# Two chained MLPs behind a small convolution: the two VectorE passes of a step put together, side work spread wider, six blocks in front

## The chip, the cores and the metric

One core of a Trainium2 chip runs the whole program. The metric is the device time of one execution in microseconds (us); smaller is better. Of the kernel before, three runs are shown (1156.45 to 1156.87 us) beside one profiled execution.

## The reference

`x` is 2 x 4096 x 192, `weight_gen` 2 x 4096 x 8 x 7, both float32. Each of the 8192 tokens gets a softmax over 7 taps in 8 heads, and a causal sum of the last 7 tokens with these taps. Two MLPs follow, each 192 to 2048 to 192 wide:

```python
w = np.exp(weight_gen - weight_gen.max(-1, keepdims=True)); w /= w.sum(-1, keepdims=True) + 1e-9
x = np.einsum('bshk,bskhg->bshg', w, x_unf).reshape(8192, 192)
h = np.maximum(x @ w_in, 0);  x = (h * h) @ w_out
h = x @ w2_in;  out = (h * np.clip(h + 3, 0, 6) / 6) @ w2_out
```

## The kernel before, in words

Every float32 operand of a matmul is split in a high part, which TensorE takes exactly, and a low part, and three products (high x high, high x low, low x high) make one result. Tokens go in 16 blocks of 512, the 2048 hidden columns in 16 tiles of 128. A *unit* is one block, one MLP and one hidden tile; two units make a *step* (`FG = 2`), eight steps one MLP of one block. `units` is the order: first `LEAD` blocks of the first MLP, then by turns one block of the second MLP and one of the first, at the end the `LEAD` blocks of the second MLP that are left. That is 32 stretches of eight steps, 256 steps.

In a step TensorE (`emit_pair`, all matmuls at L335) multiplies into `h` of the new unit pair, 9 pairs of matmuls that run side by side on the halves of the array, and mixes in the 10 pairs with which the pair of three steps earlier (`LAG = 6` units) goes through the second matrix into `accN` and `accR`. Behind it, per pair of units:

- `emit_E1` on ScalarE reads `h`: the first MLP's relu (L419) and square (L420), the second MLP's relu of h + 3 (L422). It writes `g`.
- `emit_V1` on VectorE, second MLP alone: g = min(g, 6) * h (L428).
- `emit_E2` on ScalarE: the high part `gh` of `g` (L433).
- `emit_V2` on VectorE: the low part `gl` = g - gh (L439). `g`, `gh`, `gl` and the PSUM tile `h` have two buffers each.

E1 and V1 of a pair are issued one step behind its matmuls, E2 and V2 two steps behind, and TensorE takes `gh` and `gl` in the step after that.

Besides, VectorE and ScalarE do side work. A *conversion* of a weight group (256 hidden columns, eight groups per MLP) splits the raw weights: `weight_head` (VectorE L119, then ScalarE L123, L124) and the four operations o2 to o5 of `weight_ops` (VectorE L137, L142, L149, L154; behind L142 the ScalarE casts L145, L146). A *convolution* of a block is a softmax for every second block (L204 to L220, with an exp on ScalarE, L208), thirteen products and sums (L235, L248), and a transpose (L314) whose result goes through DRAM: SyncE stores it (L318), and `from_dram` loads it as `x` (L306). Then `split_1` (ScalarE, L268) and `split_2` (VectorE, L273) make the halves `sh` and `sl`, at fixed places: six and four units ahead of the block's start. `finish` (L447) empties the accumulators. Conversions and convolutions are lists of jobs with due times. `run_jobs` hands out the next operations by estimated costs, `UNIT` per step less what is fixed; when a job is due it is issued whatever it costs. ScalarE operations that follow from a job are put off with `later` to the end of the step (`flush`).

The order within a step stands in the loop at L685 to L703:

```python
emit_E1(*units[i - FG])
emit_E2(*units[i - 2 * FG])
emit_V1(*units[i - FG])
...   # operations at fixed places, run_jobs(i)
emit_V2(*units[i - 2 * FG])
```

SyncE issues nearly all DMAs in one queue in program order; a DMA whose data is not ready keeps those behind it waiting.

Of the kernel before, what the change touches and what calls it, by code (L numbers as in the profile page):

```python
# [18 lines left out]
def conv_moe_moe2_kernel(  # L19
# [26 lines left out]
    NK = D // HP  # L46
    DR = D - P
    LAG = 6
    LEAD = 4

    xf = x.rearrange("b s d -> (b s) d")
    wf = wgen.rearrange("b s h k -> (b s) (h k)")
# [20 lines left out]
    FG = 2  # L73
# [120 lines left out]
    def load_rest():  # L194
        nc.sync.dma_start(out=wc[0][:, TB:, :], in_=w_v[:, TB:CT, :])
        nc.sync.dma_start(out=xc[0][:, PAD + TB:, :], in_=x_v[:, TB:CT, :])

    def softmax_ops(c, t0=0, t1=CT):
        e = wc[c][:, t0:t1, :].rearrange("p t (h k) -> p (t h) k", k=K)
        n = (t1 - t0) * H  # L200
        st = att.tile([P, CT * H, 2], F32, tag="pr", name="st", bufs=2)[:, 0:n, :]

        def o1():
            nc.vector.tensor_reduce(out=st[:, :, 0:1], in_=e, axis=AX.X, op=ALU.max)  # L204

        def o2():
            nc.vector.tensor_tensor(out=e, in0=e, in1=st[:, :, 0:1].to_broadcast([P, n, K]), op=ALU.subtract)
            later(lambda: nc.scalar.activation(e, e, AF.Exp))  # L208

        def o3():  # L210
            nc.vector.tensor_reduce(out=st[:, :, 1:2], in_=e, axis=AX.X, op=ALU.add)

        def o4():
            nc.vector.tensor_scalar_add(st[:, :, 1:2], st[:, :, 1:2], 1e-9)

        def o5():
            nc.vector.reciprocal(out=st[:, :, 0:1], in_=st[:, :, 1:2])

        def o6():
            nc.vector.tensor_tensor(out=e, in0=e, in1=st[:, :, 0:1].to_broadcast([P, n, K]), op=ALU.mult)  # L220

        return [(o, .45) for o in (o1, o2, o3, o4, o5, o6)]
# [44 lines left out]
    def split_1(m, b):  # L267
        nc.scalar.copy(halves(m, b)[0], xraw[m, b][:, 0:NK])  # L268

    def split_2(m, b):  # L270
        src = xraw.pop((m, b))[:, 0:NK]
        hi, lo = xs_in[m, b]
        nc.vector.tensor_tensor(out=lo, in0=src, in1=hi.bitcast(F32), op=ALU.subtract)  # L273

    def x_tile():
        return act.tile([P, NK + 1, N], F32, tag="x", name="x")
# [24 lines left out]
    def from_dram(m, b):  # L301
        Sf = xdram.pop((m, b))
        x = xraw[m, b] = x_tile()
        n = NK + m
        for h in range(2):
            nc.sync.dma_start(  # L306
                out=x[h * HP:(h + 1) * HP, 0:n], in_=Sf[0:n * HP].rearrange("(j p) n -> p j n", p=HP)
            )

    def transpose_dma(b):  # L310
        a = attn.pop(b)
        S = scr.tile([D, Q, P], F32, tag="xs", name="xs")
        aT = att.tile([P, J, TB, 32], F32, tag="pr", name="aT", bufs=2)
        nc.vector.transpose(  # L314
            out=aT.rearrange("p j t c -> p t j c"), in_=a.rearrange("p t (j c) -> p t j c", j=J)
        )
        for q in range(Q):
            nc.sync.dma_start(  # L318
                out=S[:, q, :].rearrange("(j c) n -> c j n", c=32),
                in_=aT[q * 32:(q + 1) * 32].rearrange("p j t c -> p j (t c)"),  # L320
            )
        xdram[0, b] = S.rearrange("d q n -> d (q n)")
        at.setdefault(max(unit_now[0] + 2, start_of[0, b] - 12), []).insert(0, lambda: from_dram(0, b))

    freed = []

# [88 lines left out]
    def emit_E1(m, b, f):  # L415
        ps = h_ps[m, b, f]
        g = g_sb[m, b, f] = gp.tile([P, FG, N], F32, tag="g", name="g")
        if m == 0:
            nc.scalar.activation(g, ps, AF.Relu)  # L419
            nc.scalar.activation(g, g, AF.Square)  # L420
        else:
            nc.scalar.activation(g, ps, AF.Relu, bias=3.0)  # L422

    def emit_V1(m, b, f):
        ps = h_ps.pop((m, b, f))
        if m == 1:
            g = g_sb[m, b, f]
            nc.vector.scalar_tensor_tensor(out=g, in0=g, scalar=6.0, in1=ps, op0=ALU.min, op1=ALU.mult)  # L428

    def emit_E2(m, b, f):  # L430
        g = g_sb[m, b, f]
        gh = gp.tile([P, FG, N], F32R, tag="gh", name="gh")
        nc.scalar.copy(gh, g)  # L433
        g_sb[m, b, f] = gh, g

    def emit_V2(m, b, f):
        gh, g = g_sb[m, b, f]
        gl = gp.tile([P, FG, N], F32R, tag="gl", name="gl")
        nc.vector.tensor_tensor(out=gl, in0=g, in1=gh.bitcast(F32), op=ALU.subtract)  # L439
        g_sb[m, b, f] = gh, gl  # L440
# [13 lines left out]
    def finish_1(b):  # L454
        z = zsum.pop((0, b))
        S = scr.tile([2 * P, N], F32, tag="ys", name="ys", bufs=LEAD + 1)
        for o in (1, 0):
# [73 lines left out]

    stages = [(0, b) for b in range(LEAD)]
    for b in range(LEAD, NB):
        stages += [(1, b - LEAD), (0, b)]
    stages += [(1, b) for b in range(NB - LEAD, NB)]
    units = [(m, b, f) for m, b in stages for f in range(NF)]
    NU = len(units)
    unit_of = {u: i for i, u in enumerate(units)}
    start_of = {(m, b): unit_of[m, b, 0] for m in range(2) for b in range(NB)}
# [13 lines left out]
    for u, (m, b, f) in enumerate(units):  # L553
        need.setdefault((m, f // FG), u)

    UNIT, UNIT2, AHEAD, DEBT = 4.45, 3.8, 8, 1
    COST = {0: 1.25, 1: 2.45}
    at, load = {}, {}

    def put(u, op, cost=0):  # L560
        at.setdefault(u, []).append(op)
        load[u] = load.get(u, 0) + cost
# [3 lines left out]
    def job(kind, make, due, release=0):  # L566
        jobs[kind].append([due, release, make, None, False])
# [3 lines left out]
    def weight_job(i):  # L571
        ops = weight_ops(*groups[i])
        if i + 2 < len(groups):
            ops.insert(2, (lambda: load_weights(*groups[i + 2]), 0))
        if i + 1 < len(groups):
            ops.insert(-1, (lambda: weight_head(*groups[i + 1]), .6))
        if i + 1 == len(groups):
            ops.append((lambda: freed.append(True), 0))
        return ops

    def conv_job(b):
        c, t0 = divmod(b * TB, CT)
        ops = []
        if b == 1:
            ops += softmax_ops(0, TB, CT)
        elif t0 == 0:
            ops += softmax_ops(c)
        ops += conv_ops(b)
        if t0 and b + 1 < NB:
            ops.append((lambda: load_chunk(c + 1), 0))  # L590
        ops.append((lambda: transpose_dma(b), 1))
        ops.append((lambda: ended_at.append(unit_now[0]), 0))
        return ops
# [11 lines left out]
    unit_now = [0]  # L605
# [32 lines left out]

    for i in range(1, len(groups)):
        job("w", lambda i=i: weight_job(i), need[groups[i]] - FG)  # L640
    job("a", lambda: conv_job(1), start_of[0, 1] - 10)
    for b in range(1, NB):

        if b > 1:
            rel = max(start_of[0, b - 1] + 2, end_of[0, b - 2] - 6)
            due = start_of[0, b] - (12 if b <= LEAD else 10)
            job("a", lambda b=b: conv_job(b), due, (rel, b, start_of[0, b - 1] - 8))
        put(start_of[0, b] - 6, lambda b=b: split_1(0, b))
        put(start_of[0, b] - 4, lambda b=b: split_2(0, b), 1.75)
# [14 lines left out]
    with tc.manual_schedule():  # L664
        load_chunk(0)
        load_weights(0, 0)
        load_rest()
        nc.gpsimd.memset(tiny, 0.0)
        nc.scalar.activation(tiny, tiny, AF.Exp)
        load_weights(0, 1)  # L670
        make_identity(nc, ident)
        c0 = conv_ops(0)
        steps = softmax_ops(0, 0, TB) + c0[:-2] + [(lambda: weight_head(0, 0), 0)] + c0[-2:]
        for op, _ in steps:
            op()
            flush()
        w0 = weight_job(0)

        steps = [(lambda: transpose_pe(0), 0)] + w0[1:4] + w0[:1]
        steps += [(lambda: split_pe(0), 0)] + w0[5:] + w0[4:5]  # L680
        for op, _ in steps:
            op()
            flush()

        for i in range(0, NU + LAG, FG):  # L685
            if i < NU or i in second:
                emit_pair(units[i] if i < NU else None, second.get(i))
            if 0 <= i - FG < NU:
                emit_E1(*units[i - FG])
            if 0 <= i - 2 * FG < NU:  # L690
                emit_E2(*units[i - 2 * FG])
            if 0 <= i - FG < NU:
                emit_V1(*units[i - FG])
            for u in range(i, i + FG):
                for op in at.get(u, []):
                    op()
            run_jobs(i)
            if 0 <= i - 2 * FG < NU:
                emit_V2(*units[i - 2 * FG])
            m, b, f = second.get(i - FG, (0, 0, 0))  # L700
            if f + FG == NF and (m, b) != units[-1][:2]:
                finish(m, b)
            flush()  # L703
        finish_last(NB - 1)
# [30 lines left out]
```

## Time and profile before

| | |
|---|---|
| three runs | 1156.45, 1156.47 (median), 1156.87 us |
| profiled execution | 1157.02 us, span 1155.2 us, mean granted TensorE clock 0.984 |
| TensorE busy | 1097.3 us, 95% |
| VectorE busy | 825.8 us, 71% |
| ScalarE busy | 769.9 us, 67% |
| DMA | 87.90 MB, mean 76 GB/s |

The span runs from the first to the last instruction; the profiled execution's own time lies 1.8 us above it. Busy shares are means over stages that differ: a start without matmuls, a front in which weights are converted, a long middle, and an end.

### The profile page before, as it was taken

The numbers are of one execution on the slowest core, as the hardware profiler recorded it, in microseconds if no ns is written. First come the engines' busy times: TensorE is split into PE (matmuls) and PEld (weight loads), VectorE is DVE, ScalarE is ACT, GpSimd is POOL, SyncE is SP. The second block draws the span as 40 slices with busy tenths as digits, with TensorE's granted clock in tenths as the row PEclk, the third lists the DMA queues.
The fourth block names the chain that finished last, engine by engine and source line by source line (L and its number), as shares of the span: only waits on it lengthen the run. The fifth ranks groups of instructions, "written<-read, shape, count | busy, mean of one in ns | idle before, by whom it ended". The sixth has DMA issues, their size and how long they took to land.

```text
span 1155.2 us, 23575 instructions
## 1 busy us (share of the span) xinstructions
PE 1097.3 (95%) x9722; PEld 922.9 (80%) x9722; DVE 825.8 (71%) x839; ACT 769.9 (67%) x829; POOL 3.3 (0%) x11
## 2 busy tenths in 40 slices
PE   2679999999999999999999999999999999999998
PEld 1457777788878888888888888888888888888886
DVE  8969897785777767776686857767677766366665
ACT  3677889576676757667575765757567575756553
POOL 0000000000000000000000000000000000000000
PEclk9679999999999999999999999999999999999999
DMA  5552534024113322314202241143223132022211
GB/s 137 162 127 60 168 95 114 20 65 130 37 47 93 98 60 51 87 39 139 56 28 74 53 142 37 42 96 98 60 49 90 38 84 56 28 69 51 74 42 47
DMA packets 68755, 87.90 MB, mean 76 GB/s; under 512 B 5612, under 2 KB 44396, under 8 KB 67752
## 3 DMA queue, kind: packets, MB, share of 16 engines
q1 hardware_dynamic: 68504, 86.19, 28.0%
q8 instruction: 77, 1.26, 0.5%
q14 instruction: 30, 0.25, 0.1%
q10 hardware_dynamic: 144, 0.20, 0.0%
HBM read 59.89 MB, written 26.48 MB: 75 GB/s over the span
## 4 chain that ended last, share of the span: by engine, by line
PE 76%; DVE 10%; ACT 7%; issue 3%; DMA 2%; SPq 1%; DVEq 0%; ACTq 0%
PE h L335 35%; PE accN L335 24%; PE accR L335 17%; DVE gl L439 3%; DVE pr L235 2%; ACT g L419 2%; ACT gh L433 2%; DVE a L248 2%; ACT g L420 1%; DMA st<-in_moe_w_out_dram 1%; DVE w L154 1%; DMA xs<-aT 0%; DVE hb L142 0%; ACT q L123 0%; ACT t L124 0%
## 5 line engine op out<-in xcount | busy, mean ns | idle before, releaser
L335 PE MATMUL h<-sh,w 64*128 64x512 f32 x3072 | 615.9, 381 | 19.1 <-DVE w L154 8.8
L335 PE MATMUL accN<-gh,w 64*128 64x512 f32 x2024 | 522.3, 378 | 0.3 <-ACT gh L433 0.3
L335 PE MATMUL h<-sl,w 64*128 64x512 f32 x1536 | 443.1, 380 | 0.0
L335 PEld LDWEIGHTS h<-sh,w 64*128 64x128 f32 x3072 | 386.1, 188 | 68.9 <-DVE w L154 12.3
L439 DVE TENSOR_TENSOR gl<-g,gh 128x1024 fp32r<-128x1024 f32 x256 | 312.2, 1220 | 135.3 <-ACT gh L433 135.3
L335 PEld LDWEIGHTS accN<-gh,w 64*128 64x128 f32 x2024 | 378.4, 187 | 30.0 <-ACT gh L433 1.5
L335 PE MATMUL accR<-gl,r 64*128 64x512 f32 x1012 | 311.2, 388 | 13.8 <-DVE gl L439 10.9
L335 PE MATMUL accN<-gl,w 64*128 64x512 f32 x1012 | 311.1, 388 | 0.0
L335 PE MATMUL accR<-gh,r 64*128 64x512 f32 x1012 | 301.4, 378 | 0.0
L428 DVE SCALAR_TENSOR_TENSOR g<-g,h 128x1024 f32<-128x1024 f32 x128 | 156.3, 1221 | 168.8 <-ACT g L422 168.8
L422 ACT ACTIVATE g<-h 128x1024 f32<-128x1024 f32 x128 | 131.0, 1023 | 211.6 <-DVE gl L439 145.5
L433 ACT CAST gh<-g 128x1024 fp32r<-128x1024 f32 x256 | 264.5, 1033 | 0.5 <-PE accR L393 0.4
L335 PEld LDWEIGHTS h<-sl,w 64*128 64x128 f32 x1536 | 240.6, 188 | 20.3
L335 PEld LDWEIGHTS accR<-gl,r 64*128 64x128 f32 x1012 | 181.9, 187 | 59.7 <-DVE gl L439 51.1
L419 ACT ACTIVATE g<-h 128x1024 f32<-128x1024 f32 x128 | 131.1, 1024 | 125.1 <-DVE gl L439 105.2
L335 PEld LDWEIGHTS accR<-gh,r 64*128 64x128 f32 x1012 | 189.7, 187 | 13.2
L335 PEld LDWEIGHTS accN<-gl,w 64*128 64x128 f32 x1012 | 181.7, 187 | 13.5
L420 ACT ACTIVATE g<-g 128x1024 f32<-128x1024 f32 x128 | 135.8, 1061 | 4.1
L248 DVE TENSOR_TENSOR a<-a,pr 128x768 f32<-128x768 f32 x96 | 91.2, 950 | 0.3
L235 DVE TENSOR_TENSOR pr<-xc,wc 128x768 f32<-128x768 f32 x96 | 90.3, 953 | 1.3
L273 DVE TENSOR_TENSOR sl<-x,sh 128x1536 fp32r<-128x1536 f32 x31 | 54.4, 1754 | 2.0 <-ACT sh L268 0.5
L268 ACT CAST sh<-x 128x1536 fp32r<-128x1536 f32 x31 | 45.8, 1476 | 3.4 <-DMA x<-xs 3.4
(58 smaller groups left out, 291.3 us busy)
## 6 DMA issues: line engine op xcount, KB each, us to landing
x<-ys SPq DMA_DIRECT2D x32, 512.0 KB, 6.3
x<-xs SPq DMA_DIRECT2D x30, 384.0 KB, 5.2
xc<-in_x_dram SPq DMA_DIRECT2D x7, 1344.0 KB, 7.0
ys<-z SPq DMA_DIRECT2D x32, 256.0 KB, 2.5
st<-in_moe_w_in_dram SPq DMA_DIRECT2D x32, 192.0 KB, 3.6
xs<-aT SPq DMA_DIRECT2D x60, 96.0 KB, 2.6
zq<-zs SPq DMA_DIRECT2D x60, 96.0 KB, 2.4
out_dram<-o SPq DMA_DIRECT2D x15, 384.0 KB, 2.4
```

Of the source, the lines that this page charges most:

```text
L154: nc.vector.scalar_tensor_tensor(out=out, in0=part(lo), scalar=2.0 ** -36, in1=part(sc), op0=ALU.mult, op1=ALU.mult)
L235: nc.vector.tensor_tensor(out=dst, in0=xs, in1=ws.to_broadcast([P, TB, H, G]), op=ALU.mult)
L248: nc.vector.tensor_tensor(out=acc, in0=acc, in1=pr.pop(k), op=ALU.add)
L268: nc.scalar.copy(halves(m, b)[0], xraw[m, b][:, 0:NK])
L273: nc.vector.tensor_tensor(out=lo, in0=src, in1=hi.bitcast(F32), op=ALU.subtract)
L335: return lambda: nc.tensor.matmul(ps, w[r], turns(x[r]), start=start, stop=stop)
L419: nc.scalar.activation(g, ps, AF.Relu)
L420: nc.scalar.activation(g, g, AF.Square)
L422: nc.scalar.activation(g, ps, AF.Relu, bias=3.0)
L428: nc.vector.scalar_tensor_tensor(out=g, in0=g, scalar=6.0, in1=ps, op0=ALU.min, op1=ALU.mult)
L433: nc.scalar.copy(gh, g)
L439: nc.vector.tensor_tensor(out=gl, in0=g, in1=gh.bitcast(F32), op=ALU.subtract)
```

## The change

Five edits. (1) A step's VectorE order becomes V1, V2, then side work, where V2 stood behind the side work. With it ScalarE's order becomes E2 of the old pair, then E1 of the new one, when the new pair is of the first MLP; E1, then E2, as before, when it is of the second. (2) `LEAD` is 6 instead of 4. (3) `UNIT` and `UNIT2`, the side work per step, fall from 4.45 and 3.8 to 4.0 and 3.3. (4) A convolution's due time is 12 units ahead of its block in all blocks. (5) `from_dram` is issued two steps behind the store, not one.

```diff
-    LEAD = 4
+    LEAD = 6
...
-        at.setdefault(max(unit_now[0] + 2, start_of[0, b] - 12), []).insert(0, lambda: from_dram(0, b))
+        at.setdefault(max(unit_now[0] + 2 * FG, start_of[0, b] - 12), []).insert(0, lambda: from_dram(0, b))
...
-    UNIT, UNIT2, AHEAD, DEBT = 4.45, 3.8, 8, 1
+    UNIT, UNIT2, AHEAD, DEBT = 4.0, 3.3, 8, 1
...
-    job("a", lambda: conv_job(1), start_of[0, 1] - 10)
+    job("a", lambda: conv_job(1), start_of[0, 1] - 12)
...
-            due = start_of[0, b] - (12 if b <= LEAD else 10)
+            due = start_of[0, b] - 12
...
-            if 0 <= i - FG < NU:
-                emit_E1(*units[i - FG])
-            if 0 <= i - 2 * FG < NU:
-                emit_E2(*units[i - 2 * FG])
-            if 0 <= i - FG < NU:
-                emit_V1(*units[i - FG])
+            new = units[i - FG] if 0 <= i - FG < NU else None
+            old = units[i - 2 * FG] if 0 <= i - 2 * FG < NU else None
+            if new and new[0]:
+                emit_E1(*new)
+                emit_V1(*new)
+            if old:
+                emit_E2(*old)
+                emit_V2(*old)
+            if new and not new[0]:
+                emit_E1(*new)
+                emit_V1(*new)
             for u in range(i, i + FG):
                 for op in at.get(u, []):
                     op()
             run_jobs(i)
-            if 0 <= i - 2 * FG < NU:
-                emit_V2(*units[i - 2 * FG])
```

First place: ScalarE in block 2 of the first MLP, where the second MLP's groups 0 and 1 are converted (`q`, `t`: head; `w1_1`, `r1_1`: the casts of group 1). Before:

```order
L433 CAST gh_1229<-g_1171 128x1024
L123 ACTIVATE q_1248<-q_1248 128x768
L124 COPY t_1249<-st_645 128x768
L419 ACTIVATE g_1298<-h_1183 128x1024
L420 ACTIVATE g_1298<-g_1298 128x1024
L433 CAST gh_1301<-g_1226 128x1024
L145 CAST w1_1_1305<-hb_1307 128x640
L146 CAST r1_1_1306<-hb_1307 128x2x64
L419 ACTIVATE g_1357<-h_1255 128x1024
```

Now:

```order
L433 CAST gh_1276<-g_1226 128x1024
L419 ACTIVATE g_1280<-h_1179 128x1024
L420 ACTIVATE g_1280<-g_1280 128x1024
L123 ACTIVATE q_1300<-q_1300 128x768
L124 COPY t_1301<-st_647 128x768
L433 CAST gh_1348<-g_1280 128x1024
L419 ACTIVATE g_1352<-h_1233 128x1024
L420 ACTIVATE g_1352<-g_1352 128x1024
L145 CAST w1_1_1357<-hb_1359 128x640
L146 CAST r1_1_1358<-hb_1359 128x2x64
L433 CAST gh_1409<-g_1352 128x1024
```

A step's cast to `gh` stood behind its relu and square and ahead of the side work; now it opens the step, so the side work of one step lies between its square and the next step's cast.

Second place: VectorE in the same steps of block 2. Before:

```order
L314 STREAM_TRANSPOSE aT<-a 128x4x6x32
L149 TENSOR_SCALAR q<-hb 128x768
L119 TENSOR_SCALAR q<-st 128x768
L439 TENSOR_TENSOR gl<-g,gh 128x1024
L154 SCALAR_TENSOR_TENSOR w_0_943<-t,q 128x640
L154 SCALAR_TENSOR_TENSOR r_0_944<-t,q 128x2x64
L137 TENSOR_SCALAR t<-st 128x768
L142 SCALAR_TENSOR_TENSOR hb<-st,q 128x768
L439 TENSOR_TENSOR gl<-g,gh 128x1024
```

Now:

```order
L439 TENSOR_TENSOR gl<-g,gh 128x1024
L314 STREAM_TRANSPOSE aT<-a 128x4x6x32
L149 TENSOR_SCALAR q<-hb 128x768
L119 TENSOR_SCALAR q<-st 128x768
L439 TENSOR_TENSOR gl<-g,gh 128x1024
L154 SCALAR_TENSOR_TENSOR w_0_942<-t,q 128x640
L154 SCALAR_TENSOR_TENSOR r_0_943<-t,q 128x2x64
L137 TENSOR_SCALAR t<-st 128x768
L142 SCALAR_TENSOR_TENSOR hb<-st,q 128x768
```

The rows alternate alike, but a step used to end with its `gl`, and now begins with it: the side work stands behind `gl` of its own step.

Third place: SyncE's queue where block 1's convolution is stored (`xs`) and loaded (`x`); `st` are raw weight groups, `moe` the first MLP's. Before, with group 7 as the last of them (group 6 had been issued ahead of the rows shown):

```order
L176 DMA wc_422<-in_weight_gen_dram 128x448
L177 DMA xc_421<-in_x_dram 128x2688
L318 DMA xs_433<-aT_434 32x6x128 x4
L306 DMA x_493<-xs_433 64x3x512 x2
L97 DMA st_496<-in_moe_w_in_dram 64x3x256 x2
L103 DMA st_496<-in_moe_w_out_dram 128x2x256
```

Now, with group 6 as `st_425` and group 7 as `st_498`:

```order
L176 DMA wc_361<-in_weight_gen_dram 128x448
L177 DMA xc_360<-in_x_dram 128x2688
L318 DMA xs_364<-aT_365 32x6x128 x4
L97 DMA st_425<-in_moe_w_in_dram 64x3x256 x2
L103 DMA st_425<-in_moe_w_out_dram 128x2x256
L103 DMA st_425<-in_moe_w_out_dram 128x2x128
L306 DMA x_488<-xs_364 64x3x512 x2
L97 DMA st_498<-in_moe_w_in_dram 64x3x256 x2
```

One weight group now stands between the store and the load that waits for it, and group 7 still stands behind that load.

## Rows read from the trace of the kernel before

**Rows 1.** The page: busy by engine; of a group, busy us, mean ns, idle before.

```profile
PE 1097.3 (95%) x9722; PEld 922.9 (80%) x9722; DVE 825.8 (71%) x839; ACT 769.9 (67%) x829; POOL 3.3 (0%) x11
...
L248 DVE TENSOR_TENSOR a<-a,pr 128x768 f32<-128x768 f32 x96 | 91.2, 950 | 0.3
```

**Rows 2.** Windows by stage: length, busy PE, PEld, DVE, ACT, POOL, granted clock, DMA, GB/s.

```profile
23.27:83.44 60.17, 40.46 (x245) 28.73 (x247) 50.72 (x79) 42.70 (x53) 0.00 (x0) 0.74 0.56 147
83.44:234.16 150.72, 142.10 (x1219) 114.95 (x1217) 123.61 (x140) 117.22 (x133) 0.00 (x0) 0.99 0.35 91
234.16:1042.59 808.43, 804.99 (x7298) 684.01 (x7296) 562.61 (x534) 543.81 (x569) 0.00 (x0) 1.00 0.26 70
1042.59:1136.93 94.34, 94.34 (x878) 82.76 (x876) 62.87 (x56) 52.92 (x57) 0.00 (x0) 1.00 0.19 51
```

**Rows 3.** The chain that ended last: start, length; the `h` rows open TensorE steps.

```profile
222.01 1.08 PE h L335 x10
226.12 1.08 PE h L335 x10
...
322.44 1.08 PE h L335 x10
...
324.20 0.48 PE accR L335
...
326.84 1.08 PE h L335 x10
```

**Rows 4.** Timeline of ScalarE and VectorE in one step of the first MLP.

```profile
264.98 1.02 ACT L419 ACTIVATE g<-h 128x1024 f32<-128x1024 f32 x1 [1.35 <-DVE gl L439]
266.04 1.06 ACT L420 ACTIVATE g<-g 128x1024 f32<-128x1024 f32 x1
267.00 1.03 ACT L433 CAST gh<-g 128x1024 fp32r<-128x1024 f32 x1
...
268.06 1.22 DVE L439 TENSOR_TENSOR gl<-g,gh 128x1024 fp32r<-128x1024 f32 x1 [3.17 <-ACT gh L433]
...
269.38 1.02 ACT L419 ACTIVATE g<-h 128x1024 f32<-128x1024 f32 x1 [1.35 <-DVE gl L439]
```

**Rows 5.** Waits over the whole span: us in total, times, longest.

```profile
ACT g L419 <- DVE gl L439: 105.2, 90, 3.7
```

**Rows 6.** Timeline in block 2: ScalarE and VectorE while weights are converted.

```profile
127.34 0.84 ACT L123 ACTIVATE q<-q 128x768 uint32<-128x768 uint32 x1
...
129.10 1.00 ACT L419 ACTIVATE g<-h 128x1024 f32<-128x1024 f32 x1
...
132.03 0.72 ACT L145 CAST w<-hb 128x640 fp32r<-128x640 f32 x1
...
128.61 0.82 DVE L154 SCALAR_TENSOR_TENSOR w<-t,q 128x640 fp32r<-128x640 uint32 x1
...
130.15 1.22 DVE L142 SCALAR_TENSOR_TENSOR hb<-st,q 128x768 uint32<-128x768 uint32 x1
132.16 1.22 DVE L439 TENSOR_TENSOR gl<-g,gh 128x1024 fp32r<-128x1024 f32 x1 [0.79 <-ACT gh L433]
133.30 0.55 DVE L149 TENSOR_SCALAR q<-hb 128x768 uint32<-128x768 uint32 x1
133.77 0.67 DVE L119 TENSOR_SCALAR q<-st 128x768 uint32<-128x768 uint32 x1
```

**Rows 7.** Timeline of the first block: SyncE's queue, and VectorE behind it.

```profile
54.29 2.14 SPq L318 DMA_DIRECT2D xs<-aT  x4
61.47 1.24 SPq L306 DMA_DIRECT2D x<-xs  x2
...
70.85 0.56 DVE L119 TENSOR_SCALAR q<-st 128x768 uint32<-128x768 uint32 x1 [7.85 <-DMA st<-in_moe_w_out_dram]
```

**Rows 8.** Windows in block 1: a TensorE wait, and the stretch after it.

```profile
96.97:100.91 3.94, 1.89 (x18) 1.33 (x14) 3.87 (x5) 0.61 (x1) 0.00 (x0) 1.00 0.00 1
100.91:104.32 3.41, 3.12 (x14) 2.50 (x16) 1.59 (x3) 3.05 (x4) 0.00 (x0) 0.50 0.55 115
```

## The prediction

> **What bounds the kernel now.** I read the page first, then windows by stage, then the chain and the timeline inside one step. TensorE is busy for 95% of the span, VectorE and ScalarE for 71% and 67% [rows 1]: TensorE is near its bound on the mean, and the question is where it is not. The chain gives the length of an undisturbed step: two steps open 4.10 us apart [rows 3], so a stretch of eight steps costs 32.8 us at best and 32 stretches 1050 us. Against that I hold the stages [rows 2]. The first matmul of `h` comes at 23.27. Block 0 takes 60.17, which is 27.4 too much, with the clock at 0.74. The next four stretches (blocks 1 to 3 and the second MLP's first) take 150.72, 19.5 too much. The 24 stretches after them take 808.43, 21.2 too much. The next 23 steps take 94.34, their floor, and from there, 1136.93, the last step with the drain takes 18.27 to the span's end. So 68 us are lost ahead of 1042.59, and only those can be won.
>
> **Why the long middle loses.** In the steps that are late, TensorE's steps open 4.40 apart instead of 4.10 [rows 3]. The timeline shows a ring of the same length [rows 4]: relu at 264.98, square at 266.04, cast to `gh` at 267.00, VectorE's `gl` at 268.06, and the next relu at 269.38, which waits 1.35 for that `gl`, because `gl` is the last reader of the `g` buffer that the relu overwrites. Four operations in series make 4.40, and no engine is full: ScalarE stands still at the end of every step. Over the span the relu waits 105.2 us for `gl`, in 90 steps [rows 5]. The slack of a pair of units hides the first few of these steps; after that each costs TensorE 0.30.
>
> **Edit 1, in the middle.** The cast now stands ahead of relu and square, and `gl` follows it at once. The relu then waits for a `gl` that was issued one step earlier and ahead of that step's side work. ScalarE's own order is cast, relu, square: (266.04 - 264.98) + (267.00 - 266.04) + 1.03 = 3.05 us [rows 4], below 4.10 by a microsecond, which covers `split_1` and the exp once in a while. `gl` can be done about 2.2 us after its TensorE step opens and is needed 5.8 after it (4.10 plus the 1.76 at which a step first takes it, 324.20 - 322.44 [rows 3]), so VectorE may be 3.6 us behind without harm; the largest side work of a first-MLP step in the middle is now four products and sums of a convolution, 4 x 0.95 = 3.8 if none overlaps [rows 1], and hardly more than 3.6 where they follow closely. What is late next: in the second MLP VectorE's product must be done before the step after next reuses `h`. Four of the blocks there now get two sums, one product and the transpose of a convolution in one step, four operations again, and the product behind them comes about 0.2 late. I let 1.5 us stay in all. **Middle: -19.7** (between -21.2, all gone, and -13, if each of those four also waits 2 us for its `x` load, which is two steps later than before).
>
> **Edits 2 to 4, in the front.** `LEAD = 6` gives the second MLP's eight groups five blocks (1 to 5) instead of three and a part; the number of operations stays. By VectorE's sum alone this would pay. But the same edit 1 builds a ring here. A step in which weights are converted now runs: cast, `gl`, side work on VectorE, then the ScalarE operations that need it, and behind these the next cast. Priced from starts: cast to `gl` 1.06 [rows 4], `gl` to the next operation 1.14 (133.30 - 132.16) [rows 6].
>
> - A head step adds L149 0.47 and L119 0.67 on VectorE, then L123 and L124 on ScalarE, 1.76 (129.10 - 127.34) [rows 6]: 5.10.
> - A cast step adds L154, L137 and L142, 2.76 (128.61 to the end of L142 at 131.37), then L145 and L146, about 0.95 [rows 6]: 5.9.
>
> Before, that side work ran under relu and square, and such steps took 4.4 to 4.8 (3.05 plus 1.76 on ScalarE alone). A lone one is still free: a cast may start 0.3 ahead of its TensorE step and at latest 2.1 behind it (4.10 less 0.95 to the relu less 1.02 for it), a slack of 2.4. In the changed order one step stands alone in block 1 and one in block 3; in blocks 2, 4 and 5 four to five stand in a row, with a transpose, a softmax or a `split_2` in one of each row (some 0.35 per step). Such a row lasts 4 x (5.5 + 0.35) = 23.4 against 16.4, and loses 7.0 less what slack VectorE's own lag has left, 4.6 to 7.0. I take 6 for each of three: 18. Block 1 has one step with seven products and sums and a transpose, some 7.3 us, since a convolution comes due there: its `gl` gets some 0.8 late, and `split_1`, which waits for the `x` load behind that transpose, costs some 2.7 (the store alone held the load back for 7.18 in block 0, 54.29 to 61.47 [rows 7], and the load's own time comes on top, against three steps of 4.10). Front: 18 + 3.5 = 21.5 on five blocks against 19.5 on four stretches. **+2.0** (between 5 left, -14.5, and 30, +10.5). The two blocks that go to the front leave two second-MLP stretches more at the end, where such stretches stand at their floor [rows 2]: nothing.
>
> **Block 0, edits 1 and 5.** The first `gl` now stands ahead of group 3's conversion and waits for its cast: about 1.0 of waiting and 1.14 of work ahead of weights that TensorE waits for, +2.2. The load of `x` waits in SyncE's queue for the store (54.29 to 61.47), and VectorE then waits 7.85 for group 7 behind it [rows 7]. Edit 5 puts one group between the two, but that group had been issued earlier, and group 7 still stands behind the load: the wait stays. **+2** (-6 if the wait goes, +8 if a second one comes).
>
> **Sum.** -19.7 + 2.0 + 2 = -15.7: span 1155.2 to 1139.5; the profiled execution took 1157.02, 1.8 above its span, and the median of the three runs is 0.55 below it. **1140.8 us.** About 0.2% (2.3 us) is what a measurement of this kernel tells from no change.
>
> **The rivals.**
>
> *The front is free.* VectorE was busy for 123.61 us and ScalarE for 117.22 in the four stretches [rows 2]; two first-MLP stretches more at some 26 each make (123.61 + 52) / 6 = 29 and 28 per stretch, against 32.8. So the rings may find slack that I don't see, and 5 us are left. For it: no engine is overfull. Against it: the order, in which the next cast stands behind the conversion. The Trainium skill, Perfetto Trace Analysis, section on the Tensor Engine Instruction, says that ScalarE and VectorE take their queues strictly in order; by that rule nothing behind a waiting `gl` or cast can pass it, which speaks for the ring and against this rival. Time: 1140.8 - 16.5 = **1124**. Chance 0.25.
>
> *The clock falls in the front.* In block 1 TensorE was busy for 1.89 of 3.94 us, and the next 3.41 us ran at 0.50, which is 1.2 of 2.4 GHz [rows 8]: some 1.7 us lost. If each row of conversion steps brings two such stretches, 6 x 1.7 = 10: **1151**. Chance 0.12. The Trainium skill, TensorE: Matmul & The Clock Gate, section on HAM oscillation, says that a kernel whose matmuls pause in every turn falls back to the slow clock again and again; by that rule this rival would hold. The trace is divided: the later front, though late by 15%, kept 0.99 on the mean [rows 2].
>
> *SyncE's queue (slower).* Group loads stand behind an `x` load that waits for its store. Where a conversion step reaches its group first, VectorE waits as in block 0, 7.85 [rows 7], with the next cast behind it. Edits 2 to 4 bring the rows of conversions and the stores into the same blocks. Two more such waits cost the gain (15.7); three, one per row, give 1140.8 + 23.6 = **1164**. Against it: `x` is now issued two steps behind the store, when the store has mostly landed. Chance 0.10.
>
> *The change does not do what it says.* If the relu stayed tied to the `gl` of its own step, the 4.40 ring would stay and the front be as it was: **1157**. The order speaks against it. Chance 0.04.
>
> **How the numbers follow.** Forecast 0.45; rivals 0.25, 0.12, 0.10, 0.04; the last 0.04 lies below all of them. The range 1122 to 1153 takes in the forecast with its bounds, the free front and the fallen clock, 0.82. Faster 0.86 (forecast, front, clock, and what lies below), same 0.04, slower 0.10.
>
> **What would show it.** Right: from block 6 on TensorE's steps open 4.10 apart nearly everywhere, and the relu's wait for `gl` falls from 105 us to under 20. In blocks 2, 4 and 5 steps of 5 to 6 us, TensorE waiting there on `h` (released by the relu) or `gl`, and a new wait of ScalarE's L123 and L145 for VectorE. Block 0 60 to 65 us long. Wrong: steps of 4.40 left in the middle, front blocks of 33 us, or VectorE waiting for weight loads in blocks 2 to 5.

## The result and the profile after

The changed kernel takes 1145.16 us (median of four runs, 1144.37 to 1147.65) against 1156.64 for the kernel before (four runs): ratio 0.9904, 95% interval 0.9887 to 0.9921. It is faster by 11.5 us; the prediction said 15.7. The profiled execution took 1144.37 us, its span is 1142.6.

The page of the changed kernel: the busy line, and three groups (busy us, mean ns of one, idle before, and what ended most of it).

```profile
PE 1073.3 (94%) x9722; PEld 926.7 (81%) x9722; DVE 822.4 (72%) x839; ACT 771.7 (68%) x829; POOL 3.5 (0%) x11
...
L439 DVE TENSOR_TENSOR gl<-g,gh 128x1024 fp32r<-128x1024 f32 x256 | 312.4, 1220 | 120.1 <-ACT gh L433 119.3
...
L419 ACT ACTIVATE g<-h 128x1024 f32<-128x1024 f32 x128 | 130.2, 1017 | 0.5 <-DVE gl L439 0.4
...
L248 DVE TENSOR_TENSOR a<-a,pr 128x768 f32<-128x768 f32 x96 | 91.4, 952 | 0.5
```

No operation became cheaper or rarer [rows 1]; only the waits moved. The relu (L419) waited 105.2 us for `gl` [rows 5] and now waits 0.4. TensorE's busy time fell by 24.0 us with the same 9722 matmuls. So its 95% before [rows 1] was not all work: the long middle lost 21 us although TensorE counted as busy for 804.99 of its 808.43 us [rows 2]. Losses are therefore read from step lengths below, and not from busy shares.

Windows by stage of the changed kernel: block 0; the six stretches of the front (blocks 1 to 5 and the second MLP's first); the 199 steps after them; the last step with the drain. Columns as in [rows 2].

```profile
23.11:83.86 60.75, 39.00 (x246) 27.87 (x247) 51.28 (x79) 42.93 (x54) 0.00 (x0) 0.80 0.55 146
83.86:304.77 220.91, 201.19 (x1826) 171.13 (x1824) 173.65 (x192) 171.90 (x187) 0.00 (x0) 1.00 0.31 84
304.77:1125.11 820.34, 817.76 (x7564) 715.22 (x7562) 571.48 (x536) 543.55 (x571) 0.00 (x0) 1.00 0.26 68
1125.11:1142.60 17.49, 12.59 (x82) 10.06 (x78) 7.96 (x8) 6.05 (x7) 0.46 (x2) 1.00 0.20 67
```

A stretch with no late step lasts 32.81 us here (the floor in all that follows), so the windows turn into losses. The front loses 220.91 - 6 x 32.81 = 24.0 us, where four stretches lost 19.5 [rows 2]. The 199 steps have a floor of 816.1 and lose 4.3, where the long middle lost 21.0 [rows 2] (808.43 - 24 x 32.81). Block 0 is 0.6 longer than before, the drain 0.8 shorter, the start 0.2 shorter. -16.7 + 4.5 + 0.6 - 0.8 - 0.2 = -12.6, the difference of the spans.

The same for the front alone, one window per stretch (blocks 1, 2, 3, 4, 5, and the second MLP's first):

```profile
83.86:119.67 35.81, 33.34 (x307) 28.48 (x305) 32.78 (x34) 27.37 (x30) 0.00 (x0) 1.00 0.20 49
119.67:159.44 39.77, 34.09 (x306) 28.37 (x304) 29.25 (x37) 32.07 (x37) 0.00 (x0) 1.00 0.45 124
159.44:193.20 33.76, 33.08 (x307) 28.70 (x304) 30.58 (x33) 28.41 (x30) 0.00 (x0) 1.00 0.29 75
193.20:231.51 38.31, 34.00 (x306) 28.36 (x304) 28.31 (x36) 32.47 (x37) 0.00 (x0) 1.00 0.45 129
231.51:270.21 38.70, 33.51 (x307) 28.43 (x304) 28.96 (x34) 30.75 (x35) 0.00 (x0) 1.00 0.37 92
270.21:304.77 34.56, 33.17 (x304) 28.80 (x306) 23.76 (x24) 20.83 (x23) 0.00 (x0) 1.00 0.08 26
```

Blocks 2, 4 and 5, where the conversions stand in a row, lose 7.0, 5.5 and 5.9. No engine is full in them: VectorE and ScalarE are busy for 28 to 33 of 38 to 40 us. What goes on there shows in the timeline of block 2, of ScalarE and then of VectorE, in three late steps (a cast step, a head step, a cast step):

```profile
130.36 1.04 ACT L433 CAST gh<-g 128x1024 fp32r<-128x1024 f32 x1
...
135.29 0.72 ACT L145 CAST w<-hb 128x640 fp32r<-128x640 f32 x1 [1.88 <-DVE hb L142]
...
136.12 1.04 ACT L433 CAST gh<-g 128x1024 fp32r<-128x1024 f32 x1
...
138.11 1.06 ACT L420 ACTIVATE g<-g 128x1024 f32<-128x1024 f32 x1
139.08 0.58 ACT L447 ACTIVATE z<-accR 128x512 f32<-128x512 f32 x1
139.55 0.59 ACT L447 ACTIVATE z<-accN 128x512 f32<-128x512 f32 x1
140.03 0.84 ACT L123 ACTIVATE q<-q 128x768 uint32<-128x768 uint32 x1
140.76 1.20 ACT L124 COPY t<-st 128x768 uint16<-128x768 uint16 x1
141.86 1.04 ACT L433 CAST gh<-g 128x1024 fp32r<-128x1024 f32 x1
```

```profile
131.43 1.23 DVE L439 TENSOR_TENSOR gl<-g,gh 128x1024 fp32r<-128x1024 f32 x1 [2.94 <-ACT gh L433]
...
134.08 1.17 DVE L142 SCALAR_TENSOR_TENSOR hb<-st,q 128x768 uint32<-128x768 uint32 x1
137.19 1.23 DVE L439 TENSOR_TENSOR gl<-g,gh 128x1024 fp32r<-128x1024 f32 x1 [1.94 <-ACT gh L433]
...
138.81 0.66 DVE L119 TENSOR_SCALAR q<-st 128x768 uint32<-128x768 uint32 x1
142.94 1.23 DVE L439 TENSOR_TENSOR gl<-g,gh 128x1024 fp32r<-128x1024 f32 x1 [3.47 <-ACT gh L433]
144.08 0.61 DVE L204 TENSOR_REDUCE st<-wc 128x64 f32<-128x448 f32 x1
...
149.97 1.23 DVE L439 TENSOR_TENSOR gl<-g,gh 128x1024 fp32r<-128x1024 f32 x1 [1.94 <-ACT gh L433]
```

The first turn is the ring that was forecast: cast (130.36), `gl` (131.43), side work up to L142 (134.08 to 135.25), L145 and L146 behind it (L145 waits 1.88 us for L142), and the next cast only at 136.12. It is 5.76 long instead of 4.10, and VectorE stands still for 1.94 us at its end, waiting for a cast that waits for VectorE's own side work. The second turn (136.12 to 141.86) is 5.74 long, but not by the ring alone: VectorE's side work is done at 139.47, while L123 starts at 140.03, because the two operations of `finish` (L447) stand ahead of it and ScalarE works from 135.29 to the end of this turn without a pause. A head step without `finish`, in block 4, takes 5.29 (casts at 203.32 and 208.61), and there L123 waits 0.37 us for L119. The next turn, with a softmax (L204) and, at its end, the casts L145 and L146, takes 7.0 (142.94 to 149.97). TensorE waits for the relu behind each: 1.39 us at 138.13, 1.38 at 143.88 and 2.67 at 150.91 by its rows.

### The profile page after: what moved, and what is told of

It is laid out like the page before. It is cut to its first block, busy times and chain, and to the rows that moved or that the text cites. A ratio compares the mean times of both kernels' runs of the same rounds, so it can differ in the third digit from the quotient of the medians.

```text
span 1142.6 us, 23542 instructions
## 1 busy us (share of the span) xinstructions
PE 1073.3 (94%) x9722; PEld 926.7 (81%) x9722; DVE 822.4 (72%) x839; ACT 771.7 (68%) x829; POOL 3.5 (0%) x11
## 4 chain that ended last, share of the span: by engine, by line
PE 77%; DVE 11%; ACT 4%; issue 3%; DMA 2%; SPq 2%; DVEq 0%; ACTq 0%
PE h L335 37%; PE accN L335 24%; PE accR L335 16%; DVE a L248 2%; DVE gl L439 2%; DMA st<-in_moe_w_out_dram 1%; ACT gh L433 1%; DVE pr L235 1%; DVE g L428 1%; DVE hb L142 1%; ACT t L124 1%; DVE w L154 1%; ACT g L422 1%; DVE t L137 1%; DVE aT L314 1%
## 5 line engine op out<-in xcount | busy, mean ns | idle before, releaser
L439 DVE TENSOR_TENSOR gl<-g,gh 128x1024 fp32r<-128x1024 f32 x256 | 312.4, 1220 | 120.1 <-ACT gh L433 119.3
L335 PE MATMUL accR<-gl,r 64*128 64x512 f32 x1012 | 300.6, 377 | 0.7 <-DVE gl L439 0.7
L335 PE MATMUL accN<-gl,w 64*128 64x512 f32 x1012 | 300.6, 377 | 0.0
L335 PEld LDWEIGHTS accR<-gl,r 64*128 64x128 f32 x1012 | 188.7, 187 | 14.9 <-DVE gl L439 1.4
L335 PEld LDWEIGHTS accN<-gl,w 64*128 64x128 f32 x1012 | 188.6, 186 | 13.4
L419 ACT ACTIVATE g<-h 128x1024 f32<-128x1024 f32 x128 | 130.2, 1017 | 0.5 <-DVE gl L439 0.4
L268 ACT CAST sh<-x 128x1536 fp32r<-128x1536 f32 x31 | 45.5, 1468 | 12.3 <-DMA x<-xs 12.2
```

Of the source, the lines that this page charges most:

```text
L335: return lambda: nc.tensor.matmul(ps, w[r], turns(x[r]), start=start, stop=stop)
```

## The experiments

The theory was two rings. Edit 1 opens the one of the middle, and edit 1 builds the one of the front, because `gl`, which waits for its step's cast, stands ahead of the side work. The rivals: the gain comes from spreading the side work (edits 2 to 4) and not from the order; or the loss of the front is work, not order. "Lost" is time above 32.81 us per stretch, from windows cut like those above; the front is four stretches where `LEAD` is 4 and six where it is 6, the rest is what lies between it and the last step. The kernels before that ran beside these took 1156.8 to 1156.9.

| kernel | median us | block 0 | front lost | rest lost | drain |
|---|---|---|---|---|---|
| before | 1156.64 | 60.17 | 19.5 (4) | 21.0 | 18.27 |
| changed | 1145.16 | 60.75 | 24.0 (6) | 4.3 | 17.49 |
| e1_order_only | 1152.70 | 64.53 | 32.4 (4) | 0.0 | 17.85 |
| e2_no_order | 1162.54 | 55.19 | 25.4 (6) | 23.3 | 18.33 |
| e3_gl_last | 1121.46 | 57.63 | 4.1 (6) | 4.5 | 17.47 |
| e4_load_early | 1151.43 | 67.01 | 24.4 (6) | 6.5 | 17.48 |
| e5_gl_last_unit2 | 1117.34 | 55.58 | 5.9 (6) | 0.4 | 17.48 |
| e6_gl_last_lead4 | 1130.54 | 55.98 | 14.9 (4) | 4.6 | 17.46 |
| e7_old_costs | 1150.17 | 62.53 | 32.4 (6) | 0.0 | 17.48 |
| e8_lead4 | 1148.42 | 61.08 | 26.2 (4) | 4.4 | 17.47 |
| e9_cast_last | 1218.12 | 68.71 | 67.3 (6) | 26.6 | 17.47 |
| e10_conv1_later | 1117.50 | 57.00 | 5.2 (6) | 0.4 | 17.46 |

### e1_order_only: edit 1 alone

The kernel before with the loop of the changed one, `LEAD = 4` and all costs and due times as before.

> The kernel before with edit 1 alone (the new order in a step; four blocks in front, the old job costs and due times, the x load one step behind). Theory (edit 1 ends the 4.40 ring of the middle and builds the cast, gl, conversion, cast ring in the front): the 24 middle stretches fall from 808 to about 790 us, the four front stretches stay slow or get slower, 150 to 157 us with conversion steps of 5 to 7 us; in all 1137 to 1145 us. Rival (the gain comes from six blocks in front and the wider side work): 1150 us or more, and the middle keeps steps of 4.40.

Measured: ratio 0.9962 [0.9947, 0.9977], outside the expected times and in the rival's, but without the steps of 4.40 that the rival needs. Both halves of the theory show in its windows by stage (block 0, four stretches, 215 steps):

```profile
23.11:87.64 64.53, 41.00 (x246) 28.84 (x247) 50.02 (x76) 42.34 (x53) 0.00 (x0) 0.74 0.52 138
87.64:251.33 163.69, 140.00 (x1218) 117.53 (x1216) 123.86 (x143) 118.52 (x133) 0.00 (x0) 0.97 0.31 82
251.33:1133.01 881.68, 881.68 (x8173) 773.84 (x8170) 622.38 (x588) 596.83 (x626) 0.00 (x0) 1.00 0.26 69
```

Behind the front TensorE is busy for all of 881.68 us, 215 steps of 4.10: the order alone takes away everything that the middle lost. The front takes 13 us more than before, where I had expected at most 6, and block 0 4.4 more. The order alone gives back most of its gain. Not all of the 13 is the ring: in three steps of the front the granted clock is 0.71 or 0.72 on the mean (0.97 over the four stretches).

### e2_no_order: everything but edit 1

The changed kernel with the old loop.

> The changed kernel without edit 1 (six blocks in front, lower job costs, due times and x load as changed, but the old order in a step: gl behind the side work, the cast behind relu and square). Theory: the 4.40 ring is back in the first-MLP stretches of the middle, some 15 to 18 us, while conversion steps in the front are 4.4 to 4.9 us instead of 5 to 7, so the front stretches 1 to 5 lose about 15 to 20; in all 1150 to 1158 us. Rival (the spread pays by itself): 1147 us or less.

Measured: 1.0053 [1.0036, 1.007], slower than before and 4.5 us above the expected times. The rest loses 23.3 again, half of it in steps of 4.40 and most of the other half in four steps of 6.63 where a convolution ends in the second MLP. The rival that spreading side work makes the gain falls: edits 2 to 5 without edit 1 cost 5.6 us, with it they gain 7.5 (1152.70 to 1145.16). Block 0 is the best yet, 55.19.

### e3_gl_last: `gl` behind the side work, the cast still first

In the changed kernel V2 of a first-MLP pair goes back behind the side work; ScalarE's order stays that of the change, and so does V2 of the second MLP.

```diff
             if old:
                 emit_E2(*old)
-                emit_V2(*old)
+                if old[0]:
+                    emit_V2(*old)
...
             run_jobs(i)
+            if old and not old[0]:
+                emit_V2(*old)
```

> The changed kernel with half of edit 1 taken back, for pairs of the first MLP: the cast to gh still opens ScalarE's step, but VectorE makes gl behind the side work again. Theory: the relu no longer waits for the gl of its own step, so the middle keeps its 4.10, and a conversion on VectorE no longer waits for the cast, so the front ring is cut too: conversion steps under 5 us, stretches 1 to 6 lose 5 to 12 us instead of 24; 1126 to 1134 us. Rival (the front is slow from the amount of work on ScalarE and VectorE or from weight loads, not from the ring): within 3 us of 1145.

Measured: 0.9695 [0.9681, 0.971], 24 us faster than the changed kernel and 4.5 below the expected times. Windows by stage of the front and the rest:

```profile
81.01:282.00 200.99, 198.53 (x1826) 172.05 (x1824) 172.51 (x190) 171.02 (x187) 0.00 (x0) 1.00 0.35 93
282.00:1102.58 820.58, 817.78 (x7565) 715.22 (x7562) 569.82 (x536) 543.99 (x571) 0.00 (x0) 1.00 0.26 68
```

VectorE and ScalarE do the same work in the front (172.51 and 171.02 us against 173.65 and 171.90 above), and the front loses 4.1 instead of 24.0. So its loss was order, not work. The same head step in this kernel's timeline of VectorE:

```profile
126.12 0.56 DVE L149 TENSOR_SCALAR q<-hb 128x768 uint32<-128x768 uint32 x1
128.26 0.73 DVE L119 TENSOR_SCALAR q<-st 128x768 uint32<-128x768 uint32 x1 [1.59 <-DMA st<-in_moe_w_out_dram]
128.86 1.26 DVE L439 TENSOR_TENSOR gl<-g,gh 128x1024 fp32r<-128x1024 f32 x1
```

The side work no longer waits for the cast, and `gl`, behind it, finds the cast done: no wait at all. Over the span VectorE's waits of `gl` for `gh` fall from 119.3 to 41.6 us.

### e9_cast_last: `gl` first, the cast behind relu and square

The other half of edit 1 undone: in the changed kernel the blocks `if old:` and `if new and not new[0]:` change places.

> The changed kernel with the other half of edit 1 taken back: gl still stands ahead of the side work on VectorE, but ScalarE does relu and square of the new pair ahead of the cast of the old one, as before. Theory: then relu, square, cast and gl are in series again, so the 4.40 ring of the middle is back (some 15 us or more), and a conversion step strings cast, gl, conversion, its ScalarE work, relu and square together, 7 to 8 us instead of 5 to 6, which is some 25 us more in the front; 1170 to 1195 us. Rival (it is gl's place on VectorE that ends the middle's ring): the middle stays at 4.10 and the time within 10 us of 1145.

Measured (two runs): 1.0531 [1.051, 1.0552]. The direction was right, the size was not: 73 us above the changed kernel, where 25 to 50 were expected. The steps of 4.40 are back in the middle (they make about half of the 26.6 lost there, steps of 4.6 to 5.3 the rest), the relu again waits 100.8 us for `gl`, and most conversion steps in blocks 2 and 4 last 6.4 to 8.7. Its timeline in one of them, ScalarE, then VectorE:

```profile
323.60 0.72 ACT L145 CAST w<-hb 128x640 fp32r<-128x640 f32 x1 [3.65 <-DVE hb L142]
...
324.44 1.01 ACT L419 ACTIVATE g<-h 128x1024 f32<-128x1024 f32 x1
325.48 1.06 ACT L420 ACTIVATE g<-g 128x1024 f32<-128x1024 f32 x1
326.45 1.03 ACT L433 CAST gh<-g 128x1024 fp32r<-128x1024 f32 x1
```

```profile
327.51 1.23 DVE L439 TENSOR_TENSOR gl<-g,gh 128x1024 fp32r<-128x1024 f32 x1 [3.94 <-ACT gh L433]
```

Relu and square now lie inside the front's ring. So it is the cast's place on ScalarE that opens the middle, with `gl` in either place (e1, e3), and `gl` ahead of the side work that closes the front. The front needs both: six stretches lose 25.4 with neither operation moved (e2_no_order), 4.1 with the cast first alone, 24.0 with both first, 67.3 with `gl` first alone. One half of edit 1 carries the gain, the other most of the loss.

### e4_load_early: edit 5 undone

`from_dram` one step behind the store again (`2 * FG` back to `2`).

> The changed kernel with edit 5 taken back: the x load one step behind its store. Theory: the place of this load decides little; 1143 to 1148 us. Rival (SyncE's queue, the load holding weight groups back while it waits for its store): over 1150 us, with VectorE waiting for weight loads in the front.

Measured: 0.9953 [0.9938, 0.9968], 6.3 us slower than the changed kernel; a miss, since I had held edit 5 for nearly nothing; the rival's time and its wait for weights came out. Of the 8.9 us between the two profiled executions 6.3 lie in block 0 (67.01 against 60.75), and 2.2 in the rest, where one late `x` load costs more. SyncE's queue and VectorE there, in e4_load_early:

```profile
58.28 1.24 SPq L306 DMA_DIRECT2D x<-xs  x2
59.62 1.25 SPq L97 DMA_DIRECT2D st<-in_moe_w_in_dram  x2
...
67.54 0.56 DVE L119 TENSOR_SCALAR q<-st 128x768 uint32<-128x768 uint32 x1 [6.05 <-DMA st<-in_moe_w_out_dram]
```

and in the changed kernel:

```profile
55.16 1.26 SPq L97 DMA_DIRECT2D st<-in_moe_w_in_dram  x2
...
58.26 1.24 SPq L306 DMA_DIRECT2D x<-xs  x2
60.88 1.25 SPq L97 DMA_DIRECT2D st<-in_moe_w_in_dram  x2
...
61.34 0.62 DVE L119 TENSOR_SCALAR q<-st 128x768 uint32<-128x768 uint32 x1
```

The load of `x` goes out at the same time in both, when the store has landed. But in the changed kernel a weight group (group 6) is issued in the 3.1 us ahead of it, and that is the group VectorE takes next; the following group it takes at 68.08, also without a wait.

### e7_old_costs and e8_lead4: edits 3 and 2 undone

`UNIT, UNIT2` back to 4.45 and 3.8; and, in another kernel, `LEAD` back to 4.

> The changed kernel with edit 3 taken back (job costs 4.45 and 3.8). Theory: the four second-MLP stretches with a late product lose nothing any more (4.2 us in the changed kernel), and the front keeps its conversion steps of 5 to 7 us, since their number is the same; 1138 to 1145 us. Rival (the lower costs are what makes the front bearable): 1150 us or more.

> The changed kernel with edit 2 taken back (four blocks in front). Theory: the conversion steps lie closer together, so a lone step's slack is used more rarely: the front loses 30 to 34 us on four stretches as in e1_order_only, against 24 on six; 1148 to 1156 us. Rival (the ring costs the same per step wherever it stands, six blocks give nothing): within 3 us of 1145.

Measured: e7_old_costs 0.9939 [0.9925, 0.9954], a miss, with a time in the rival's range; e8_lead4 0.9924 [0.9909, 0.9938], the time as expected, but with 26.2 lost in the front where the theory had 30 to 34. The lower costs are worth 5.0 us by the medians, 6.0 between the profiled executions: they cost 4.3 in the rest, where e7_old_costs loses nothing (so it is the spread that makes four operations meet in one second-MLP step), and spare 8.4 in the front and 1.8 in block 0. With the old costs blocks 2 and 4 have six late steps each, where the changed kernel has three or four; they reach 7.3, and the clock falls in two of each six. Below are block 2 of e7_old_costs and the last late step of its block 4, and then the step of the changed kernel that comes behind its 7.03 in block 2:

```profile
120.48:164.85 44.37, 37.34 (x306) 30.76 (x304) 31.62 (x40) 34.06 (x39) 0.00 (x0) 0.92 0.48 129
236.62:242.51 5.89, 5.89 (x38) 4.91 (x40) 5.75 (x9) 5.51 (x6) 0.00 (x0) 0.71 0.00 0
```

```profile
150.91:155.23 4.32, 4.32 (x38) 3.52 (x38) 4.18 (x8) 4.29 (x5) 0.00 (x0) 1.00 0.00 0
```

Both of these steps follow a TensorE wait of 2.67 us in a step of 7.0, and the lower clock makes the one 1.6 us longer. So a part of the 8.4 is the clock and not the ring; how much in all, the runs don't tell.

`LEAD = 6` is worth 3.3 us in the changed kernel, about the scatter of its runs.

### e5_gl_last_unit2, e6_gl_last_lead4, e10_conv1_later: what is left to win

The first two are e3_gl_last with one edit each, `UNIT2` 3.8 and `LEAD = 4`; the third is e5_gl_last_unit2 with block 1's convolution due 10 units ahead instead of 12. That is the part of edit 4 that concerns block 1; the part that concerns blocks 7 to 15 was not undone by itself in any run.

> The kernel of e3_gl_last with the second job cost back at 3.8 (3.3 there), which puts the transposes of blocks 8, 10, 12 and 14 two steps earlier, into the first step of a second-MLP stretch, where less of a convolution is left. Theory (those four stretches lose 4.4 us because VectorE's product comes late behind the end of the convolution, and because ScalarE then waits for the x load): they come down to 32.8 us each, 1116 to 1119 us. Rival (the loads of x themselves are late, whatever the place of the transpose): 1121 us, ScalarE still waiting for x.

> The kernel of e3_gl_last with four blocks in front instead of six. Theory: with the ring cut, what is left in the front is the amount of work: 16 conversion steps of 4.8 us on ScalarE in three blocks instead of five, so stretches 1 to 4 lose 8 to 14 us against 4 in e3_gl_last; 1125 to 1132 us. Rival (six blocks pay nothing once the ring is cut): within 2 us of 1121.

> The kernel of e5_gl_last_unit2 with the first block's convolution due ten units ahead of block 1 instead of twelve, so that its end no longer stands ahead of weight group 4. Theory (VectorE has the same work in block 0, and weights, the x load and the next weight groups only change places): the step of 17 us in block 0 falls to about 11 and the ones behind it grow; 1113 to 1121 us. Rival (the conversion of group 4 behind the convolution is what block 0 waits for): 1112 us or less.

All three times landed in their ranges (the front of e6_gl_last_lead4 lost 14.9, just above its 8 to 14). e5_gl_last_unit2 is the best version, 1117.34 us, 0.9661 [0.9645, 0.9677] against before, and beats both kernels. The 199 steps of its rest:

```profile
281.57:1098.03 816.46, 816.46 (x7564) 715.54 (x7562) 571.34 (x536) 543.76 (x571) 0.00 (x0) 1.00 0.26 68
```

That is TensorE's floor. e6_gl_last_lead4 (0.9768 [0.9754, 0.9783]) shows that six blocks in front are worth 9 us once the ring is open: with four, the second MLP's first stretch loses 8.3 by itself. e10_conv1_later moves block 0's longest step from 17.1 to 11.2 us, but the next two become 9.8 and 9.5: 0.966 [0.9644, 0.9676], no gain. What e5_gl_last_unit2 still loses lies mostly in block 0, some 23 us above a stretch's floor, and 5.9 in the front.

## Why the prediction was right, and where it was off

The sign, the range and the two mechanisms of the rings held: 1145.16 lies in 1122 to 1153, 4.4 above the forecast. Two smaller terms, block 0 and block 1, came near by luck.

**Edit 1 in the middle: mechanism right, 2.8 mis-sized.** I let 1.5 us stay in the four second-MLP stretches with a convolution's end; 4.3 stayed. They lose 2.6, 0.6, 0.5 and 0.6. What I had kept for the bound happened: all four wait for their `x` load, three of them 2.1 us, and ScalarE's slack hides that; the fourth (the earliest, for block 8) waits 4.08, and this shows. Edit 5 is not the cause: with it undone that load waits for its store all the same, ScalarE waits 4.73 us for it, and the stretch loses 4.9 (e4_load_early). ScalarE there, then VectorE, in the changed kernel:

```profile
430.66 1.48 ACT L268 CAST sh<-x 128x1536 fp32r<-128x1536 f32 x1 [4.08 <-DMA x<-xs]
432.04 1.02 ACT L422 ACTIVATE g<-h 128x1024 f32<-128x1024 f32 x1
```

```profile
433.09 1.22 DVE L428 SCALAR_TENSOR_TENSOR g<-g,h 128x1024 f32<-128x1024 f32 x1 [5.06 <-ACT g L422]
```

The step there takes 6.12. The product that I had 0.2 us late costs some 0.45 in each of the four, a step of 4.45 and one of 4.20 by TensorE's starts. That part comes from edit 3: with the old costs the four operations don't meet in one step, and nothing is lost (e7_old_costs).

**The front: the rows of conversions as priced, block 1 by luck.** Forecast 6 for each of three rows, measured 7.0, 5.5 and 5.9; a head step priced at 5.10 took 5.29, a cast step priced at 5.9 took 5.76. Block 1 was forecast at 3.5 and measured 3.0, but not by the mechanism that I gave it: 2.7 of it was `split_1` waiting for its `x` load, and in the changed kernel L268 follows the square at 111.49 without a wait. In its place stands a turn of the ring, which I had held to be free where a conversion step stands alone. The conversion comes behind the convolution's end and the late `gl`, and L145 waits 4.41 us for it (at 104.42). The 0.8 for the late `gl` itself was right (TensorE waits 0.67 at 102.81). Five blocks together 22.3 against 21.5. Two things I had at nothing: block 3, whose lone conversion step costs 0.9, and the last late step, which falls into the second MLP's first stretch (5.76, 1.75 lost in all). That makes the front +4.5 where I had +2.0.

I also had no price for the front under edit 1 alone. By the runs it loses 32.4 with edit 1 alone and 32.4 again with the old costs, in both with some steps at a lower clock: edit 3, and edit 2 a little, are what made the front of edit 1 bearable.

**Block 0: the sum near by luck, one term wrong and one too small.** Forecast +2, measured +0.6. I wrote that the 7.85 wait for group 7 [rows 7] stays, as group 7 still stands behind the load. It went. In the changed kernel group 6 is the one that would stand behind the load (e4_load_early waits 6.05 for it), and edit 5 lets it out ahead; group 7 follows the load at 60.88 and is taken at 68.08, 7.2 us later, where before VectorE was there at 70.85 - 7.85 = 63.0. I had the place of the groups in the queue, but not the time at which VectorE comes to them. e4_load_early puts 6.3 us on edit 5. The other term was right where I put it, but it was not all: the step in which `gl` stands ahead of group 3's conversion takes 8.66 against 6.50 before, the 2.2 that I took. The block's last two steps, which I left out, take 9.10 and 5.84 against 5.92 and 4.44 without edit 1 (e2_no_order); in the first of them `gl` at 71.90 waits 2.34 us for its cast, with a conversion behind it, as in the front. In all block 0 is 5.6 shorter without edit 1 (55.19 against 60.75) and 4.4 longer with it alone (e1_order_only). Two errors of opposite sign.

**The drain, not foreseen.** It is 17.5 us instead of 18.3. In both kernels the last `gl` but one and the transpose L490 of the output stand together on VectorE; before, the transpose (0.97, at 1143.44) was first, and the `gl` followed at 1144.33. The changed kernel:

```profile
1131.64 1.22 DVE L439 TENSOR_TENSOR gl<-g,gh 128x1024 fp32r<-128x1024 f32 x1
1132.78 0.97 DVE L490 STREAM_TRANSPOSE o<-zq 128x768 f32<-128x768 f32 x1
```

It is edit 1 again: 18.33 without it, 17.5 to 17.9 in every kernel with V2 ahead of fixed work in the second MLP.

**The rivals.** *The front is free* (1124) was right that no engine is full: VectorE and ScalarE are busy for 173.65 / 6 = 28.9 and 28.7 us per stretch, as that rival had it. The order barred it: with `gl` behind the side work the time is 1121.46. The Trainium skill's rule that ScalarE and VectorE take their queues strictly in order (Perfetto Trace Analysis, section on the Tensor Engine Instruction) is what the 3.47 us wait at 142.94 shows: VectorE has side work behind that `gl` and does none of it, though the input of the first of it (L204 at 144.08) had landed at 126.18. *The clock falls in the front*: the granted clock is 1.00 in all six stretches, although TensorE waits 1.4 to 2.7 us per late step; so the rival fell for this kernel. It was no empty rival: with the old costs the clock does fall (0.71 in four late steps of e7_old_costs, behind waits of 2.00 to 2.96 us). I leaned on the Trainium skill (TensorE: Matmul & The Clock Gate, section on HAM oscillation) further than the page goes: the kernel that falls back in every turn there has pauses that each outlast the matmul work of a turn. Here a late step holds 4.1 us of matmuls beside a shorter wait, so the page's case is not this one, and the traces show both outcomes. *SyncE's queue*: no wait of VectorE for a weight load is left in the changed kernel's list of waits; e4_load_early shows that the mechanism was real and edit 5 its cure.

## What to carry to other kernels

When two engines hand tiles to each other in a fixed order every step, write down the ring that the order makes (who waits for whom, up to the next reuse of a buffer or the next turn of the queue), and put the operation that others wait for first on the engine that makes it. An operation that must itself wait goes behind the work that need not wait. Here the first was the cast and the second was `gl`: with the changed kernel's spread of side work, moving both forward gave 17 us (e2_no_order to the changed kernel), moving the cast forward and leaving the first MLP's `gl` behind gave 41 (to e3_gl_last), and moving `gl` alone cost 56 (to e9_cast_last). A load that must wait for a store holds everything behind it in its queue, so issue late what waits, and early what doesn't.

## What the runs showed of the hardware that I had not expected

- Late steps alone do not bring the granted clock down, and the length of TensorE's wait does not tell when it falls: behind a wait of 2.67 us the next step ran at 1.00 in the changed kernel (150.91) and at 0.71 on the mean in e7_old_costs (236.62), where a wait of 2.00 did the same (154.86). Block 2 as a whole is at 1.00 in the changed kernel (TensorE busy for 34.09 of 39.77 us) and at 0.92 in e7_old_costs (37.34 of 44.37, the same matmuls, 3.25 us more of busy time). Before, a wait of 2.34 us in block 1 was followed by a stretch at 0.50, which is 1.2 GHz [rows 8]. What decides between the two was not tried.
- A store through DRAM and its load back vary: over the changed kernel's span the trace shows 1.8 to 4.5 us from issue to landing for the stores `xs` (median 2.0), and 4.2 to 6.9 for the loads `x` of them (median 5.4). Of the four like stretches, one has its load issued 5.3 us behind the store (418.81 to 424.10), another 3.4 (552.61 to 556.04), and this makes the 4.08 and the 2.1 above. What slows a store down was not tried.
